# Contiguous x pieces, logit spectra stored by frequency and read back in whole rows, and three more weight tiles, in a Fourier layer with a soft mixture of experts

## The chip, the core and the metric

One core of a Trainium2 chip runs the program. The metric is the device time of one execution in microseconds, median of several runs. TensorE (PE in the profile; its weight loads are PEld), VectorE (DVE), ScalarE (ACT) and GpSimd (POOL) compute; SyncE (SP) issues nearly all DMAs, in program order, from one queue. Sixteen DMA engines move the data.

## What is computed

```python
X = np.fft.rfft(x, axis=1)                      # x: 8 batches, 2496 tokens, 256 channels
Yr = Xr @ w_r - Xi @ w_i + b_r
Yi = Xr @ w_i + Xi @ w_r + b_i
Y  = soft_threshold(Yr, 0.01) + 1j * soft_threshold(Yi, 0.01)
y  = np.fft.irfft(Y, n=2496, axis=1)            # all 19968 tokens from here on
logits = y @ phi                                # 32 slots: 8 experts, 4 slots each
d = softmax(logits, over tokens); slot_input = d.T @ y
slot_out[e] = relu(slot_input[e] @ w1[e]) @ w2[e]   # w1: 256x1024, w2: 1024x256 per expert
out = softmax(logits, over slots) @ slot_out
```

## The kernel before

The length 2496 is 39 times 64, and the transform is done in two factors. For each batch, `a_unit` (L322) loads x in pieces of a few columns on 120 partitions, splits each piece in a high and a low part (`xh` on ACT or DVE, `xl` on POOL) and multiplies by the 39-point matrix; the result goes through `ast` to a DRAM scratch `adr` and comes back turned round as `ap` (`load_ap`, L383). `f2` does the 64-point part, `lin_k` and `lin_y` the channel matrices, then the soft threshold gives `rt`. There are 40 such steps, five groups of four frequencies for each of eight batches, and TensorE is kept busy with step s while the other engines prepare step s+1. In time units of the program a step is 4, a batch 20, and `TB` = 166 is the start of the tail after the last step; every piece of work is a generator that yields its due time, and the program text of each engine is written in the order of those times (`heapq`, L750 to L759). So each engine works in a fixed order, and an instruction that waits holds back all that stands behind it on its engine.

The inverse transform of the output is never formed. Instead the logits are found in the frequency domain: `tp_p` (L484) multiplies the thresholded spectrum by `phi`, 32 values per frequency, and collects them in `p_sb`. `c_stages` (L604) then does, for each of batches 0 to 6:

1. `pg` = the inverse 64-point matrix `sinv` times `p_sb`, copied by ACT to `g_sb`: 128 partitions by 20 frequencies by 32 slots.
2. one DMA writes `g_sb` to a DRAM scratch `gd`, laid out as 64 tokens by 40 (real or imaginary part and frequency) by 32 (L618 and L619).
3. four DMAs read `gd` as `gp`, 120 partitions (three groups of tokens, times 40) by 22 by 32: two of 40x22 pieces, one of 40x20 and one of 40x2 pieces, every piece being 32 numbers or 128 bytes (L622 to L633). The third group has 20 tokens of its own, and its last two columns repeat its first two.
4. `halves` (L578) splits `gp` in two halves: `chpL` on ACT, `clpL` on DVE, and then three products by the 39-point matrix `m2` on TensorE give `pL`, which ACT copies to `L`, the logits by token. In batch 6 and in the last batch there is no split, and TensorE reads `gp` itself.
5. from `L`: the running maximum (`mx`, `pm`, `pb`), the exponentials `ee`, the way back to the frequencies (`pe`, `ea`, DMA to `ed`, two DMAs back as `eb`, `pd`, `dd`), and the weighted sum `pr` over the spectra `T`, which gives the slot inputs.

`last_chain` (L924) is the same for batch 7, without TensorE work to hide it: `g_sb` is written in three pieces of 12, 4 and 4 frequencies as they come (L927 to L936). Then the slot inputs go through the experts (`hps`, `po`; weights `w`), and 78 blocks of output are made (`pq`, `ost`).

The weights of the experts are 32 tiles of 512 KB, loaded by `load_w` (L843) in the order of the table `wl` in `PLAN` (L143): each entry is a due time relative to `TB` and a letter for the pool that the tile takes: `r` and `a` reuse tiles of the loads, `t` is a tile of the tail pool `tw` (10 tiles, `NTA` from `"nw"`, L148), `x` and `T` are pairs of half tiles that reuse working tiles, `h` are tiles of the pool `hl`.

All DMAs named here are issued by SP, and SP waits in line: `gp` is not issued before `gd` has landed, and what stands behind `gp` (the next `xr` and `adr`) not before `gp` is issued.

Of the kernel before, what the change touches and what calls it, by code (L numbers as in the profile page):

```python
# [11 lines left out]
F32 = mybir.dt.float32  # L12
# [18 lines left out]
GP = 2  # L31
# [18 lines left out]
def _constants():  # L50
    n1 = np.arange(N1)
    k1 = np.arange(K1)
    a39 = 2 * np.pi * (np.outer(n1, k1) % N1) / N1
    c39, s39 = np.cos(a39), np.sin(a39)
    s39[:, 0] = 0.0
    a64 = 2 * np.pi * (np.outer(np.arange(N2), np.arange(N2)) % N2) / N2
    q = np.outer(np.arange(N2), np.arange(N2)) % N2
    c64, s64 = np.cos(a64), np.sin(a64)
    c64[(q == 16) | (q == 48)] = 0.0
    s64[(q == 0) | (q == 32)] = 0.0  # L60

# [26 lines left out]
    smov = smov.reshape(128, K1 + 1, 64)
    smov = np.concatenate([smov[:, : KG + 1], smov[:, :1], smov[:, KG + 1 :]], axis=1).reshape(128, -1)
    sinv = suni[np.arange(128).reshape(2, N2).T.reshape(-1)].T  # L90
    sgn = np.ones((2, N2, K1))
    sgn[1] = sig.T
    sgn = sgn.reshape(128, K1)
    dsc = sgn * wk[None, :]

    ident = np.eye(128)
    dmask = np.tile(np.eye(32), (4, 4))
    f1a = f1.reshape(P1, R, 2, NGRP, KG).transpose(0, 3, 2, 4, 1).reshape(P1, Q1)
    f1 = f1.reshape(P1, R, 2 * K1).transpose(0, 2, 1).reshape(P1, Q1)
# [12 lines left out]
    return {k: np.ascontiguousarray(v.astype(np.float32)) for k, v in out.items()}
# [27 lines left out]
    "to": 0.7,  # L140
    "ws": [-29, -28.9, -28.8, 2],
    "late": {'6': {'cms': [19.75, 19.71, 860.75, 862, 864, 865], 'pd': [20.36, 20.37], 'pr': [31.55, 31.6, 31.65, 31.7, 31.75], 'pL': [5.4, 5.8], 'pm': 6.875, 'pb': 7.325, 'pe': [8.75, 9.75], 'pg': [0.875, 1.275], 'fr': {'sinv': 0, 'm2': 0, 'f1': 0, 'suni': 0}}, '5': {'pg': [1.1, 1.8], 'pL': [4.95, 5.75], 'pm': 6.8, 'pb': 7.15, 'pe': [9.2, 9.9], 'pd': [13.8, 14.8], 'pr': [15.0, 17.25, 19.5, 21.75, 24.0]}, '4': {'pr': [18.4, 20.49, 24.49, 28.49, 32.49]}},
    "T_": {'wl': [[-45, 'r'], [-44, 'r'], [-43, 'r'], [-31.0, 't'], [-30.7, 't'], [-29.4, 't'], [-27.6, 't'], [-27.8, 't'], [-11, 'a'], [-10.3, 'a'], [-9.6, 'a'], [-7.5, 'x'], [-6.4, 'x'], [1.11, 'x'], [1.07, 'h'], [1.08, 'h'], [1.09, 'h'], [1.1, 'h'], [1.11, 'h'], [13.55, 'h'], [13.1, 'h'], [13.6, 'h'], [13.6, 'h'], [13.61, 't'], [13.61, 't'], [13.61, 't'], [13.61, 't'], [13.61, 't'], [13.7, 'T'], [13.7, 'T'], [13.7, 'T'], [13.7, 'T']], 'cl': 16, 'cp': 46.5, 'ct': 46.6, 'du': [[-4.5, 0], [-2.4, 0], [1.2, 0]], 'd1': [5, 2, 4, 0, 0, 0], 'cm': [19.9, 19.91, 19.92, 25, 25.1, 25.2], 'cm7': [18, 20, 22, 23, 25, 27], 'ye': 0.2, 'te': [[5.6, 0.2], [5.5, 0.4]], 'pg': [-7, -3.25, -0.35], 'yt': 0.5, 'wr': -30.6, 'tp': [0, 0.9, 1.05, 0.5], 'tt': [[-0.4, 0.5, 0.6, 0.7, 0.8], [12, 12.1, 12.2, 12.3, 12.4]], 'z': 13.55, 'th': [0.1, 0.12], 'tl': [0.2, 0.25]},  # L143
    "f1": [1.5, 2.15],
    "kw": [[-40, 9]],
    "ap1": 1.85,
    "f0": 0.2,
    "nw": [3, 10, 9],  # L148
    "te": 'A',
    "tp": [0.5, 1.0, 1.9, 1.8],  # L150
    "tt": [2, 2.5],
# [29 lines left out]
def fourier_soft_moe_kernel(ctx: ExitStack, tc: tile.TileContext, t: dict, out: bass.AP):  # L181
    nc = tc.nc
# [3 lines left out]
    dr = ctx.enter_context(tc.tile_pool(name="dr", bufs=2, space=bass.MemoryType.DRAM))  # L186
# [46 lines left out]
    def sp(**kw):  # L233
        tc.keep_in_program_order(nc.sync.dma_start(**kw))  # L234
# [13 lines left out]
    def split(dst_h, dst_l, src, eh, el):  # L248
        copy(eh, dst_h, src)
        el.tensor_tensor(out=dst_l, in0=src, in1=dst_h.bitcast(F32), op=ALU.subtract)  # L250

    def load_x(i):
        if i >= len(xorder) or xorder[i] in xrs:
            return
        b, g = xorder[i]
        ng = min(xc, G - g)
        xr = wtile([PX, xc, D], F32, "xr", f"xr{b}_{g}")
        sp(out=xr[:, :ng, :], in_=x[b, :, g : g + ng, :])
        xrs[(b, g)] = xr

    def load(name, shape, pool=cons, eng=None):
# [316 lines left out]
    def halves(n, t0, times, out, const, fr, src, evac):  # L578
# [13 lines left out]
        for h in range(2):  # L592
# [8 lines left out]
            yield t0 + times[h] + 0.25  # L601
            evac(h, out[1](ps))

    def c_stages(b):  # L604
        ct_ = "ps"
        K_ = dict(PLAN, **PLAN["late"].get(str(b), {}))
# [8 lines left out]
            lambda h, ps: A.copy(out=g_sb[:, h * 10 : h * 10 + 10, :].rearrange("p k s -> p (k s)"), in_=ps),  # L615
        )
        yield t0 + K_["pg"][1] + 0.35
        gd = dr.tile([N2, 2 * K1, S], F32, tag="gd", name=f"gd{b}")  # L618
        sp(out=gd.rearrange("n (c k) s -> (n c) k s", c=2), in_=g_sb)  # L619
        yield t0 + K_["pg"][1] + 0.9  # L620
        gp = wtile([Q1, G, S], F32, "gp", f"gp{b}")
        for r in range(R):  # L622
            ge = 22 if r < 2 else 20
            p0 = r * 2 * K1
            sp(
                out=gp[p0 : p0 + 2 * K1, :ge, :],
                in_=gd[22 * r : 22 * r + ge].rearrange("g k s -> k g s"),
            )
            if ge < G:
                sp(  # L630
                    out=gp[p0 : p0 + 2 * K1, ge:, :],
                    in_=gd[22 * r : 22 * r + G - ge].rearrange("g k s -> k g s"),
                )  # L633
# [290 lines left out]
    def last_chain():  # L924
        b = B - 1
        for (k0, k1), tk in zip(((0, 12), (12, 16), (16, 20)), T_["pg"]):
            ks = slice(k0, k1)  # L927
            n = (k1 - k0) * S
            yield TB + tk
            if k0 == 0:  # L930
                g_sb = wtile([128, K1, S], F32, "g7", f"g_sb{b}")
                gd = dr.tile([N2, 2 * K1, S], F32, tag="gd", name=f"gd{b}")
            ps = psum("pf", f"pg{b}_{k0}")
            mm(out=ps[:, :n], lhsT=sinv, rhs=psb[b][:, ks, :], start=True, stop=True)
            A.copy(out=g_sb[:, ks, :].rearrange("p k s -> p (k s)"), in_=ps[:, :n])
# [3 lines left out]
        for r in range(R):
            ge = 22 if r < 2 else 20  # L940
            p0 = r * 2 * K1
            sp(
                out=gp[p0 : p0 + 2 * K1, :ge, :],
                in_=gd[22 * r : 22 * r + ge].rearrange("g k s -> k g s"),
            )
            if ge < G:
                sp(
                    out=gp[p0 : p0 + 2 * K1, ge:, :],
                    in_=gd[22 * r : 22 * r + G - ge].rearrange("g k s -> k g s"),
                )  # L950
# [310 lines left out]
```

## Time and profile before

| | |
|---|---|
| median of 3 runs | 580.69 us (577.52 to 581.72) |
| the profiled execution | 575.19 us |
| its span, first to last instruction | 573.4 us |
| busy: PE, DVE, ACT, POOL | 528.8, 419.3, 298.6, 281.0 us |
| mean granted TensorE clock | 0.971 |
| DMA | 118.55 MB, 207 GB/s over the span |

The profile's page shows the span in forty slices of 14.3 us. The stretch table gives, for a window, each engine's busy time, the DMA engines' mean busy share and the rate. The timeline lists instructions by start, with a bracket that tells how long the engine was idle before and what ended that. The chain of waits follows the work that ended last back to its start. DMA issues stand in the timeline as SPq with the time that SP took to issue them; when one has landed is seen from the instruction that waited for it.

### The profile page before, as it was taken

What the parts mean: (1) busy time and instruction counts of PE and PEld (TensorE: products, weight loads), DVE (VectorE), ACT (ScalarE), POOL (GpSimd) and SP (SyncE); (2) the same over time, 40 slices, a digit from 0 to 9 for tenths busy, and PEclk for the clock granted to TensorE, in tenths of its full rate; (3) what the DMA queues carried; (4) which work ended last, traced back from release to release, by engine and by line L of the source; (5) the groups of instructions that cost most, each with busy time, mean ns of one, the idle gap of its engine ahead of it and who ended that gap; (6) DMA issues with size and microseconds to landing.
All of it is one profiled execution on the core that took longest, in us unless ns stands there. A gap on an engine that the chain in (4) does not pass through costs nothing.

```text
span 573.4 us, 11788 instructions
## 1 busy us (share of the span) xinstructions
PE 528.8 (92%) x4358; PEld 447.4 (78%) x4358; DVE 419.3 (73%) x837; ACT 298.6 (52%) x650; POOL 281.0 (49%) x258
## 2 busy tenths in 40 slices
PE   8668999999999999999999999998899989799894
PEld 4357999989898879889988888897687767367673
DVE  0254988789979897989689977986776764247783
ACT  4334555667566656665665656553333333037662
POOL 0035778667676666658655865773445412000100
PEclk9887999999999999999999999998989999999897
DMA  8779878667776858775787577866624489969898
GB/s 241 235 259 241 198 162 175 156 171 178 205 176 178 173 154 204 170 180 156 177 196 187 151 179 185 238 184 193 164 80 102 121 199 298 369 218 363 330 374 352
DMA packets 92884, 118.55 MB, mean 207 GB/s; under 512 B 46802, under 2 KB 68624, under 8 KB 92828
## 3 DMA queue, kind: packets, MB, share of 16 engines
q1 hardware_dynamic: 92572, 116.73, 73.0%
q10 hardware_dynamic: 256, 1.08, 0.5%
q8 instruction: 34, 0.56, 0.4%
q14 instruction: 22, 0.18, 0.1%
HBM read 68.42 MB, written 49.38 MB: 205 GB/s over the span
## 4 chain that ended last, share of the span: by engine, by line
PE 65%; DMA 14%; DVE 12%; ACT 3%; issue 2%; SPq 2%; POOL 0%; ACTq 0%; DVEq 0%; POOLq 0%
PE py L240 15%; PE px L240 10%; PE pq L240 8%; PE pk L240 7%; PE pa L240 7%; PE pt L530 4%; DMA gp<-gd 3%; DMA gd<-g_sb 3%; PE pr L240 3%; DMA ap<-adr 2%; SPq L234 2%; PE pc L1065 2%; DMA eb<-ed 2%; DMA xr<-in_x 2%; DVE mx L177 1%
## 5 line engine op out<-in xcount | busy, mean ns | idle before, releaser
L177 POOL TENSOR_TENSOR rt<-ut,rt 128x512 f32<-128x512 f32 x79 | 111.7, 1414 | 26.5 <-DVE rt L177 22.0
L177 POOL TENSOR_TENSOR xsl<-xsm,xsh 128x256 fp32r<-128x256 f32 x77 | 59.4, 772 | 107.3 <-DVE xsh L177 72.5
L177 POOL TENSOR_TENSOR xl<-xr,xh 117x512 fp32r<-117x512 f32 x73 | 98.4, 1349 | 21.8 <-ACT xh L177 13.8
L240 PE MATMUL px<-smov,ap 128*128 128x128 f32 x640 | 86.8, 280 | 5.7 <-DMA ap<-adr 3.9
L240 PEld LDWEIGHTS px<-smov,ap 128*128 128x128 f32 x640 | 81.5, 195 | 11.6 <-issue 4.7
L177 ACT COPY ast<-pa 120x512 f32<-120x512 f32 x86 | 50.6, 588 | 69.7 <-PE pa L240 68.1
L177 ACT CAST xth<-px 128x512 fp32r<-128x512 f32 x80 | 46.9, 586 | 74.0 <-PE py L240 38.2
L177 DVE SCALAR_TENSOR_TENSOR ut<-py,pk,k 128x256 f32<-128x256 f32 x160 | 69.5, 475 | 16.7 <-PE py L240 12.4
L177 DVE TENSOR_TENSOR xtl<-px,xth 128x512 fp32r<-128x512 f32 x80 | 54.6, 683 | 24.7 <-ACT xsm L177 22.6
L240 PE MATMUL py<-xth,nwsh 128*128 128x256 f32 x160 | 54.0, 337 | 0.0
L177 DVE TENSOR_SCALAR rt<-ut 128x512 f32<-128x512 f32 x69 | 53.3, 772 | 0.5
L240 PE MATMUL pk<-xsh,w_rh 128*128 128x256 f32 x160 | 49.3, 308 | 2.0 <-DVE xsh L177 2.0
L530 PE MATMUL pt<-pk,rt 128*128 128x128 f32 x320 | 45.9, 273 | 0.9 <-DVE dd L177 0.6
L177 ACT COPY T<-pt 128x512 f32<-128x512 f32 x70 | 42.0, 599 | 9.0 <-PE pt L530 7.0
L240 PE MATMUL pk<-xsl,w_rh 128*128 128x256 f32 x160 | 46.2, 289 | 0.0
L240 PE MATMUL pk<-xsh,w_rl 128*128 128x256 f32 x160 | 46.1, 288 | 0.0
L240 PE MATMUL py<-xtl,wdh 128*128 128x256 f32 x160 | 45.3, 283 | 0.0
L240 PE MATMUL py<-xth,wdl 128*128 128x256 f32 x160 | 45.2, 283 | 0.0
L240 PE MATMUL py<-xth,nwsl 128*128 128x256 f32 x160 | 45.2, 283 | 0.0
L240 PE MATMUL py<-xth,wdh 128*128 128x256 f32 x160 | 45.2, 282 | 0.0
L240 PE MATMUL py<-xtl,nwsh 128*128 128x256 f32 x160 | 45.1, 282 | 0.0
L240 PE MATMUL pq<-rhs,ct 128*128 128x512 f32 x156 | 43.1, 416 | 0.3 <-DVE ost L177 0.3
(186 smaller groups left out, 1245.8 us busy)
## 6 DMA issues: line engine op xcount, KB each, us to landing
ap<-adr SPq DMA_DIRECT2D x76, 256.0 KB
out<-ost SPq DMA_DIRECT2D x37, 512.0 KB
xr<-in_x SPq DMA_DIRECT2D x35, 480.0 KB
adr<-ast SPq DMA_DIRECT2D x20, 720.0 KB
w<-in_moe_w SPq DMA_DIRECT2D x25, 512.0 KB
adr<-ast SPq DMA_DIRECT2D x8, 480.0 KB
w<-in_moe_w SPq DMA_DIRECT2D x14, 256.0 KB
x<-in_x SPq DMA_DIRECT2D x11, 240.0 KB
```

What stands on the lines that cost most here:

```text
L177: return lambda *a, **k: self.tc.keep_in_program_order(f(*a, **k))
L234: tc.keep_in_program_order(nc.sync.dma_start(**kw))
L240: tc.keep_in_program_order(nc.tensor.matmul(**kw))
L530: tc.keep_in_program_order(nc.tensor.transpose(out=out, in_=in_, identity=identity))
L1065: nc.tensor.transpose(out=pc[:, i * P1 : (i + 1) * P1], in_=chls[b][x][:, 2 * (r + i) : 2 * (r + i) + 2].rearrange("p g h s -> p (g h s)") ...
```

## The change

Three things are changed together.

**x in DRAM.** Before, x lay as 120 rows of 22 columns by 256 for each batch, so that a piece of 4 columns is 120 rows of 4 KB, 22 KB apart. Now each piece lies by itself, without gaps; the DMAs have the same rows and the same bytes.

**gd and gp.** `gd` now is laid out part, frequency, token, slot. Two DMAs write it, one for each part, in pieces of 128 bytes (64 partitions by 20 pieces); in the last batch that is six DMAs for three. A row of `gd` (one part and frequency, 64 tokens) is contiguous, so `gp` is read in two DMAs of whole rows: one for the first two groups of tokens (2 by 40 rows of 704 numbers, into 80 partitions) and one for the third group (40 rows of 640 numbers). The third group stands first in `gp` (`m2` and `sinv` are permuted to fit), and its two repeated columns are copied on chip by ACT (`gp_wrap`), due 0.91 units before the logits' products, and 0.1 units before them in the last batch.

**Weights.** The pool `tw` has 13 tiles for 10; the SBUF comes from a smaller descriptor scratch. Three `t` loads are added at -24, -22 and -20; the two `x` loads at -7.5 and -6.4 are gone, three `x` loads stand at 1.12, 1.13 and 13.55, and some `h`, `t` and `T` loads behind them change places.

```diff
-    m2 = m2.reshape(Q1, P1)
+    m2 = m2[[2, 0, 1]].reshape(Q1, P1)
...
-    "nw": [3, 10, 9],
+    "nw": [3, 13, 9],
...
+    def x_piece(b, g, n):
+        return x[b, g * PX * D : (g + n) * PX * D].rearrange("(p g d) -> p g d", p=PX, d=D)
...
-        sp(out=xr[:, :ng, :], in_=x[b, :, g : g + ng, :])
+        sp(out=xr[:, :ng, :], in_=x_piece(b, g, ng))
...
+    def gd_write(gd, g_sb, k0, k1):
+        for c in range(2):
+            sp(out=gd[c, k0:k1].rearrange("k n s -> n k s"), in_=g_sb[c * N2 : c * N2 + N2, k0:k1, :])
+
+    def gp_read(gp, gd):
+        rows = gd.rearrange("c k n s -> (c k) (n s)")
+        q = 2 * K1
+        sp(
+            out=gp[q:].rearrange("p g s -> p (g s)"),
+            in_=rows[:, : 2 * G * S].rearrange("q (r x) -> r q x", r=2),
+        )
+        sp(out=gp[:q, : G - 2, :].rearrange("p g s -> p (g s)"), in_=rows[:, 2 * G * S :])
+
+    def gp_wrap(gp):
+        A.copy(out=gp[: 2 * K1, G - 2 :, :], in_=gp[: 2 * K1, :2, :])
...
-        gd = dr.tile([N2, 2 * K1, S], F32, tag="gd", name=f"gd{b}")
-        sp(out=gd.rearrange("n (c k) s -> (n c) k s", c=2), in_=g_sb)
+        gd = dr.tile([2, K1, N2, S], F32, tag="gd", name=f"gd{b}")
+        gd_write(gd, g_sb, 0, K1)
         yield t0 + K_["pg"][1] + 0.9
         gp = wtile([Q1, G, S], F32, "gp", f"gp{b}")
-        for r in range(R):
...
+        gp_read(gp, gd)
         L = wtile([P1, G, S], F32, "L", f"L{b}")
+        yield t0 + K_["pL"][0] - PLAN["cl"][0] - 0.01
+        gp_wrap(gp)
...
-            sp(out=gd.rearrange("n (c k) s -> (n c) k s", c=2)[:, ks, :], in_=g_sb[:, ks, :])
+            gd_write(gd, g_sb, k0, k1)
...
+        yield TB + 6.9
+        gp_wrap(gp)
         yield TB + 7
```

SP around the round trip of batch 0, before and with the change (`ap_4` is a load of the running step, `xr_4` a piece of x, `adr_601` a write of the first factor):

```order
L234 DMA gd_1290<-g_sb_1178 128x640
L234 DMA ap_4_1315<-adr_182 64x4x256 x2
L234 DMA gp_1326<-gd_1290 40x22x32 x2
L234 DMA gp_1326<-gd_1290 40x20x32
L234 DMA gp_1326<-gd_1290 40x2x32
L234 DMA xr_4_1332<-in_x 120x1024
L234 DMA adr_601<-ast_18_1295 120x1024
```

```order
L234 DMA gd_1290<-g_sb_1178 64x20x32 x2
L234 DMA ap_4_1316<-adr_182 64x4x256 x2
L234 DMA gp_1327<-gd_1290 80x1x704
L234 DMA gp_1327<-gd_1290 40x640
L234 DMA xr_4_1331<-in_x 120x1024
L234 DMA adr_601<-ast_18_1296 120x1024
```

One write became two, four reads became two, and the order around them is the same. Batches 1 to 6 differ in the same way.

SP in the last batch, before and with the change, from the read of batch 6's `eb` to that of batch 7's `gp` (`w` are weight tiles):

```order
L234 DMA eb_6370<-ed_6353 64x20x32 x2
L234 DMA w_0_6425<-in_moe_w 128x512
L234 DMA w_1_6426<-in_moe_w 128x512
L234 DMA gd_6432<-g_sb_6431 128x384
L234 DMA w_0_6439<-in_moe_w 128x512
L234 DMA w_1_6440<-in_moe_w 128x512
L234 DMA gd_6432<-g_sb_6431 128x128 x2
L234 DMA gp_6540<-gd_6432 40x22x32 x2
```

```order
L234 DMA eb_6376<-ed_6359 64x20x32 x2
L234 DMA gd_6434<-g_sb_6433 64x12x32 x2
L234 DMA gd_6434<-g_sb_6433 64x4x32 x4
L234 DMA gp_6541<-gd_6434 80x1x704
L234 DMA gp_6541<-gd_6434 40x640
```

The two weight tiles between the writes are gone from here, and three writes became six. A third weight load, which stood between the `ed` write and the `eb` read of the last batch, now stands behind that read.

ACT in batch 6, before and with the change, around the new copy (`lg_1` and `L` feed TensorE's next products and the logits):

```order
L177 COPY xsm_3_1_6188<-px_3_1_6169 128x256 [waits Pool_49]
L177 COPY lg_1_6209<-pq_1_6193 128x128 [waits PE_49]
L177 COPY L_6120<-pL_0_6220 117x352 [waits PE_49]
L177 COPY L_6120<-pL_1_6223 117x352 [waits PE_49]
L177 CAST xth_4_0_6249<-px_4_0_6227 128x512 [waits PE_49,Activation_49]
```

```order
L177 COPY xsm_3_1_6193<-px_3_1_6174 128x256 [waits Pool_49]
L177 COPY gp_6122<-gp_6122 40x64 [waits DMAHW4_49]
L177 COPY lg_1_6215<-pq_1_6199 128x128 [waits PE_49]
L177 COPY L_6125<-pL_0_6226 117x352 [waits PE_49]
L177 COPY L_6125<-pL_1_6229 117x352 [waits PE_49]
L177 CAST xth_4_0_6255<-px_4_0_6233 128x512 [waits PE_49,Activation_49]
```

The copy waits for a DMA and stands ahead of `lg_1`. In batches 0 to 5 it stands straight ahead of the casts `chpL`. Nothing else moves on ACT, and nothing on DVE, POOL and TensorE but which weight tile has two halves.

More of the change, by code (lines that the diff above doesn't have):

```diff
@@ L89, in _constants @@
     smov = np.concatenate([smov[:, : KG + 1], smov[:, :1], smov[:, KG + 1 :]], axis=1).reshape(128, -1)
-    sinv = suni[np.arange(128).reshape(2, N2).T.reshape(-1)].T
+    sinv = suni.T
     sgn = np.ones((2, N2, K1))
@@ L142 @@
     "late": {'6': {'cms': [19.75, 19.71, 860.75, 862, 864, 865], 'pd': [20.36, 20.37], 'pr': [31.55, 31.6, 31.65, 31.7, 31.75], 'pL': [5.4, 5.8], 'pm': 6.875, 'pb': 7.325, 'pe': [8.75, 9.75], 'pg': [0.875, 1.275], 'fr': {'sinv': 0, 'm2': 0, 'f1': 0, 'suni': 0}}, '5': {'pg': [1.1, 1.8], 'pL': [4.95, 5.75], 'pm': 6.8, 'pb': 7.15, 'pe': [9.2, 9.9], 'pd': [13.8, 14.8], 'pr': [15.0, 17.25, 19.5, 21.75, 24.0]}, '4': {'pr': [18.4, 20.49, 24.49, 28.49, 32.49]}},
-    "T_": {'wl': [[-45, 'r'], [-44, 'r'], [-43, 'r'], [-31.0, 't'], [-30.7, 't'], [-29.4, 't'], [-27.6, 't'], [-27.8, 't'], [-11, 'a'], [-10.3, 'a'], [-9.6, 'a'], [-7.5, 'x'], [-6.4, 'x'], [1.11, 'x'], [1.07, 'h'], [1.08, 'h'], [1.09, 'h'], [1.1, 'h'], [1.11, 'h'], [13.55, 'h'], [13.1, 'h'], [13.6, 'h'], [13.6, 'h'], [13.61, 't'], [13.61, 't'], [13.61, 't'], [13.61, 't'], [13.61, 't'], [13.7, 'T'], [13.7, 'T'], [13.7, 'T'], [13.7, 'T']], 'cl': 16, 'cp': 46.5, 'ct': 46.6, 'du': [[-4.5, 0], [-2.4, 0], [1.2, 0]], 'd1': [5, 2, 4, 0, 0, 0], 'cm': [19.9, 19.91, 19.92, 25, 25.1, 25.2], 'cm7': [18, 20, 22, 23, 25, 27], 'ye': 0.2, 'te': [[5.6, 0.2], [5.5, 0.4]], 'pg': [-7, -3.25, -0.35], 'yt': 0.5, 'wr': -30.6, 'tp': [0, 0.9, 1.05, 0.5], 'tt': [[-0.4, 0.5, 0.6, 0.7, 0.8], [12, 12.1, 12.2, 12.3, 12.4]], 'z': 13.55, 'th': [0.1, 0.12], 'tl': [0.2, 0.25]},
+    "T_": {'wl': [[-45, 'r'], [-44, 'r'], [-43, 'r'], [-31.0, 't'], [-30.7, 't'], [-29.4, 't'], [-27.8, 't'], [-27.6, 't'], [-24, 't'], [-22, 't'], [-20, 't'], [-11, 'a'], [-10.3, 'a'], [-9.6, 'a'], [1.07, 'h'], [1.08, 'h'], [1.09, 'h'], [1.1, 'h'], [1.11, 'h'], [1.12, 'x'], [1.13, 'x'], [13.55, 'x'], [13.6, 'h'], [13.6, 'h'], [13.6, 'h'], [13.6, 'h'], [13.61, 't'], [13.61, 't'], [13.61, 't'], [13.61, 't'], [13.61, 't'], [13.7, 'T']], 'cl': 16, 'cp': 46.5, 'ct': 46.6, 'du': [[-4.5, 0], [-2.4, 0], [1.2, 0]], 'd1': [5, 2, 4, 0, 0, 0], 'cm': [19.9, 19.91, 19.92, 25, 25.1, 25.2], 'cm7': [18, 20, 22, 23, 25, 27], 'ye': 0.2, 'te': [[5.6, 0.2], [5.5, 0.4]], 'pg': [-7, -3.25, -0.35], 'yt': 0.5, 'wr': -30.6, 'tp': [0, 0.9, 1.05, 0.5], 'tt': [[-0.4, 0.5, 0.6, 0.7, 0.8], [12, 12.1, 12.2, 12.3, 12.4]], 'z': 13.55, 'th': [0.1, 0.12], 'tl': [0.2, 0.25]},
     "f1": [1.5, 2.15],
@@ L273, in load_x0 @@
         xr = wtile([PX, GP, D], F32, "T", f"x0_{g}")
-        sp(out=xr, in_=x[0, :, g : g + GP, :])
+        sp(out=xr, in_=x_piece(0, g, GP))
         x0.append(xr[:P1])
@@ L617, in c_stages @@
         yield t0 + K_["pg"][1] + 0.35
-        gd = dr.tile([N2, 2 * K1, S], F32, tag="gd", name=f"gd{b}")
-        sp(out=gd.rearrange("n (c k) s -> (n c) k s", c=2), in_=g_sb)
+        gd = dr.tile([2, K1, N2, S], F32, tag="gd", name=f"gd{b}")
+        gd_write(gd, g_sb, 0, K1)
         yield t0 + K_["pg"][1] + 0.9
         gp = wtile([Q1, G, S], F32, "gp", f"gp{b}")
-        for r in range(R):
[L623 to L633, printed above, removed]
+        gp_read(gp, gd)
         L = wtile([P1, G, S], F32, "L", f"L{b}")
+        yield t0 + K_["pL"][0] - PLAN["cl"][0] - 0.01
+        gp_wrap(gp)
         yield from halves(
@@ L931, in last_chain @@
                 g_sb = wtile([128, K1, S], F32, "g7", f"g_sb{b}")
-                gd = dr.tile([N2, 2 * K1, S], F32, tag="gd", name=f"gd{b}")
+                gd = dr.tile([2, K1, N2, S], F32, tag="gd", name=f"gd{b}")
             ps = psum("pf", f"pg{b}_{k0}")
@@ L935, in last_chain @@
             A.copy(out=g_sb[:, ks, :].rearrange("p k s -> p (k s)"), in_=ps[:, :n])
-            sp(out=gd.rearrange("n (c k) s -> (n c) k s", c=2)[:, ks, :], in_=g_sb[:, ks, :])
+            gd_write(gd, g_sb, k0, k1)
         yield TB + 1
         gp = wtile([Q1, G, S], F32, "gp", f"gp{b}")
[L939 to L950, printed above, removed]
+        gp_read(gp, gd)
         L = wtile([P1, G, S], F32, "L", f"L{b}")
         mx = wtile([P1, 4, S], F32, "mx", f"mx{b}")
+        yield TB + 6.9
+        gp_wrap(gp)
         yield TB + 7
@@ L1211, in _prep @@
     rows = np.arange(PX) % P1
-    arrays["x"] = np.asarray(inputs["x"])[:, _tokens()[rows]]
+    xt = np.asarray(inputs["x"])[:, _tokens()[rows]]
+    arrays["x"] = np.stack([
+        np.concatenate([xt[b, :, g : g + n].reshape(-1) for g in range(0, G, n)])
+        for b, n in enumerate([GP] + [2 * GP] * (B - 1))
+    ])
     for nm in ("moe_w1", "moe_w2"):
@@ L1250 @@
     )
-    nc = _bacc.Bacc("TRN2", target_bir_lowering=False, num_devices=1)
+    nc = _bacc.Bacc("TRN2", target_bir_lowering=False, num_devices=1, dynamic_dma_scratch_size=1024)
     t = {
```

## The prediction

> **What bounds the kernel now.** I read the page first, then the stretch table, then the timelines of the two round trips that the change rewrites, and last the chain of waits for the head.
>
> ```profile
> span 573.4 us, 11788 instructions
> PE 528.8 (92%) x4358; PEld 447.4 (78%) x4358; DVE 419.3 (73%) x837; ACT 298.6 (52%) x650; POOL 281.0 (49%) x258
> ```
>
> TensorE is busy for 92%. Where TensorE has no gaps, a transfer matters only through what makes TensorE wait, so the stages have to be told apart.
>
> ```profile
> 0.00:60.00 60.00, 47.66 (x227) 34.28 (x228) 21.56 (x46) 24.93 (x47) 16.63 (x21) 0.89 0.86 244
> 60.00:107.00 47.00, 47.00 (x420) 43.39 (x419) 39.86 (x79) 27.06 (x60) 35.77 (x32) 1.00 0.71 164
> 107.00:127.00 20.00, 19.19 (x166) 17.27 (x165) 15.71 (x33) 11.91 (x26) 11.74 (x12) 1.00 0.74 184
> 380.00:405.00 25.00, 22.16 (x189) 19.79 (x189) 17.72 (x39) 11.14 (x26) 11.63 (x13) 0.93 0.59 161
> 405.00:436.00 31.00, 28.45 (x247) 24.17 (x249) 23.22 (x49) 9.57 (x24) 15.00 (x16) 0.89 0.51 135
> 462.00:513.00 51.00, 43.54 (x440) 28.28 (x439) 21.89 (x51) 13.71 (x34) 3.65 (x9) 1.00 0.90 286
> ```
>
> Each row gives the window, its length, the busy time of PE, PEld, DVE, ACT and POOL, the granted clock, the DMA share and GB/s. TensorE idles 12.3 us in the first 60, 0.8 around batch 0's round trip (107 to 127), 2.8 around batch 5's (380 to 405) and 7.5 in the tail (462 to 513); between these it has nothing to give back. So a later `gp` in batches 0 to 4 costs TensorE what goes beyond its slack there, and a faster `gp` gains nothing.
>
> **The round trip in batch 0.** SP's timeline, then the part of the full timeline that `gp` releases:
>
> ```profile
> 107.23 0.35 SPq L234 DMA_DIRECT2D gd<-g_sb  x1
> 111.23 3.32 SPq L234 DMA_DIRECT2D gp<-gd  x4
> 115.03 0.41 SPq L234 DMA_DIRECT2D adr<-ast  x1
> 120.98 1.24 SPq L234 DMA_DIRECT2D ap<-adr  x2
> 135.25 0.32 SPq L234 DMA_DIRECT2D ed<-ea  x1
> 138.09 1.38 SPq L234 DMA_DIRECT2D eb<-ed  x2
> ```
>
> ```profile
> 116.31 0.88 ACT L177 CAST chpL<-gp 120x352 fp32r<-120x352 f32 x2 [0.82 <-DMA gp<-gd]
> 117.09 0.58 ACT L177 CAST xth<-px 128x512 fp32r<-128x512 f32 x1
> 117.93 0.41 PE L240 MATMUL pL<-chpL,m2h 120*117 120x352 f32 x1
> 118.50 0.29 PE L240 MATMUL py<-xth,nwsh 128*128 128x256 f32 x1
> ```
>
> The write takes 4.0 us until SP may issue the reads, the reads 5.1 until ACT starts. ACT already waits 0.8 for them, TensorE does not: it needs `chpL` at 117.93, and a cast takes half of 0.88, so the slack is 1.6 less 0.5, or 1.1 us. Behind the cast on ACT stand `xth`, `xsm` and `T`; TensorE needs `xth` soon after `pL`, so they have about the same slack.
>
> **The price of the new transfers.** The rates come from stretches in which one kind of transfer is alone:
>
> ```profile
> 441.50:442.50 1.00, 1.00 (x13) 0.61 (x6) 0.46 (x2) 0.00 (x0) 0.61 (x1) 1.00 0.86 135
> 475.00:480.00 5.00, 4.38 (x28) 3.19 (x26) 2.49 (x9) 2.07 (x6) 0.00 (x0) 1.00 1.02 389
> 4.00:8.00 4.00, 4.00 (x12) 2.24 (x12) 0.00 (x0) 1.17 (x2) 0.00 (x0) 1.00 0.94 288
> 35.50:37.00 1.50, 1.50 (x15) 1.50 (x14) 0.88 (x2) 0.12 (x1) 0.89 (x1) 1.00 0.74 280
> ```
>
> In the first, `gp`'s 128-byte pieces move: 135 / (0.86 x 16) = 9.8 GB/s for a busy engine. In the second, whole 4 KB rows of weights: 389 / (1.02 x 16) = 23.8.
>
> *Write.* 327,680 bytes in 128-byte pieces over 16 engines take 327.7 / (16 x 9.8) = 2.1 us, against 0.86 in today's rows of 2,560 bytes: +1.2. The second issue hides behind the data. This takes the price of a 128-byte read for a write, which no row here shows; below, today's 0.86 (no loss), and above, twice the read's price, 4.2.
>
> *Read.* A `gp` DMA has a fixed part: `ed<-ea` lands 2.84 after its issue, with 337,920 bytes on at most 15 engines (120 rows), 0.95 us; that leaves 1.9. An issue with three dimensions, as `ap`'s, takes 0.6 for 0.3. What decides is over how many engines the first read's 225,280 bytes go. No view shows a DMA's engines one by one; the bounds are 16 engines, 0.6 us, and one, 9.5. The nearest row is the last one above: there `adr` is written in DMAs of 72 rows, more are queued, and the engines are busy to 0.74 only, which is twelve of sixteen, the largest number up to 16 that divides 72; weights, with 128 rows, reach 1.02. The count of the outermost dimension thus sets the number of engines. The new read's source has 2 outermost (2 by 40 rows) and its destination 80; a share has to be whole on both sides, so I take two engines: 225.3 / (2 x 23.8) = 4.7 us. The second read (40 rows, so ten engines) includes these two, behind the first: 10.2 KB each, 0.4. Together 1.9 + 0.3 + 4.7 + 0.4 = 7.3 against 5.1: +2.2.
>
> On this the Trainium skill has a rule, in "DMA: Bandwidth & Descriptors", section "Why a DMA increments its semaphore by 16 and not by 1": the number of engines is the largest up to 16 that divides the slowest dimension, other than one, of both access patterns. The 0.74 agrees for 72 rows; that both sides count, and that 2 against 80 gives two, no row of this run shows. By the rule the read's data takes the 4.7 us, and with all engines it would take 0.6.
>
> *Copy.* ACT copies 40x64 once both reads are there:
>
> ```profile
> L177 ACT COPY zrow<-dd 1x128 f32<-1x128 f32 x8 | 2.4, 294 | 4.3 <-DVE dd L177 4.3
> ```
>
> +0.3. So `chpL` starts 1.2 + 2.2 + 0.3 = 3.7 us later. Less the slack of 1.1, TensorE waits 2.6 at `pL`; I give back 0.5, since VectorE and ACT catch up meanwhile and later waits shrink. 2.1 for each of batches 0 to 4: **+10.5**. On the two engines that read, the following `adr` is held up too, and `ap` behind it (120.98), by up to 2 us; the wait at `pL` covers that, and without this cover it would be paid. SP itself waits 1.2 longer for the write, but issues two reads in 1.0 us for four in 3.3, so that `xr` and `adr` leave it earlier than now.
>
> **Batches 5 to 7.** From SP's and TensorE's timelines:
>
> ```profile
> 380.90 0.35 SPq L234 DMA_DIRECT2D gd<-g_sb  x1
> 381.31 0.42 SPq L234 DMA_DIRECT2D adr<-ast  x1
> 383.15 4.83 SPq L234 DMA_DIRECT2D gp<-gd  x4
> 439.78 2.67 SPq L234 DMA_DIRECT2D gp<-gd  x4
> 464.87 0.99 SPq L234 DMA_DIRECT2D gd<-g_sb  x2
> 468.41 2.85 SPq L234 DMA_DIRECT2D gp<-gd  x4
> 484.00 1.39 SPq L234 DMA_DIRECT2D eb<-ed  x2
> ```
>
> ```profile
> 390.63 0.64 PE L240 MATMUL pL<-chpL,m2h 120*117 120x352 f32 x1 [2.38 <-ACT chpL L177]
> 444.43 0.82 PE L240 MATMUL pL<-gp,pk 120*117 120x352 f32 x2
> 447.33 0.91 PE L240 MATMUL px<-smov,ap 128*128 128x128 f32 x6 [0.58 <-DMA ap<-adr]
> 473.38 1.41 PE L240 MATMUL pL<-gp,pk 120*117 120x352 f32 x4 [2.37 <-DMA gp<-gd]
> 490.37 1.31 PE L240 MATMUL pd<-eb,pk 128*128 128x320 f32 x4 [3.08 <-DMA eb<-ed]
> ```
>
> Batch 5 has no slack: TensorE waits 2.4 already, since the reads stand behind an `adr` write. Read data today is 337.9 / (10 x 9.8) = 3.4 behind it, then 5.1: +1.7, with write and copy **+3.2**. Batch 6: read 4.65 today, 7.3 then, +2.65, write +1.2, copy +0.3; the 0.58 at `px` is swallowed: **+3.6**. The copy also holds `lg_1` on ACT, but its product stands behind `pL` on TensorE. Batch 7: the last piece is ready at about 465.5, but six issues of 0.6 have to leave SP, so the last write lands 0.7 later; read 4.97 to 7.3, copy 0.3: **+3.3**.
>
> **Weights.** The earlier loads go into the stretch from 405 to 436, where the DMA engines are busy to 0.51, at no cost; their products are not waited for now. A 512 KB load before `eb` in batch 7 is gone, 524 / 381 = 1.4 us of every engine; `eb` needs 5.7 from its second issue to `pd`, and I take **-0.5** (0 to -1.4). The two tiles gone before `gd` leave the writes issue-bound.
>
> **Head.** The chain of waits:
>
> ```profile
> 4.79 7.01 DMA x<-in_x
> 11.82 9.63 DMA xr<-in_x
> 21.59 3.61 PE pa L240 x4
> 39.45 4.11 DMA ap<-adr
> 43.70 2.04 PE px L240 x8
> ```
>
> The head is a queue of transfers up to 43.70. x alone moves at 288 GB/s with share 0.94 (4 to 8): 19.1 for a busy engine, against 23.8 for the gapless weights. The rows are alike, so the 22 KB between them is what differs. Ahead of `ap` at 39.45 stand 11 pieces of 240 KB and three of 480 KB, 4.18 MB: 14.5 us at 288, 11.7 at 23.8 x 15 = 357: **-2.8** (0, if the gap is not the cause, to -4.5, if what follows on SP moves up too). Later x pieces are hidden by TensorE.
>
> **Sum.** 10.5 + 3.2 + 3.6 + 3.3 - 0.5 - 2.8 = +17.3 on the span of 573.4 and the execution of 575.2. That one lies 5.5 below the median of the runs, 580.69; I add the sum to the median: **598.0 us**.
>
> **Rivals.** *The first read goes wide.* If ten or more engines share it, the round trip takes 1.9 + 0.3 + 0.6 to 0.9 and the second issue, about 3.5 for 5.1; that pays for the write and the copy, TensorE's slack takes the rest, and the head and `eb` are left: -3.3, about 577, a little faster. It decides as soon as the read lands before about 3.7 us. For it: 80 partitions on the destination's side. Against it: the outer 2.
>
> *Half is hidden.* Two engines, but TensorE's slack in batches 0 to 4 reaches to the next need of `L` and `xth`, and only 1 us is paid in each, 2 in batches 5 to 7: 5 + 6 - 3.3 = +7.7, 588. For it: ACT is 52% busy. Against it: the engines' orders are fixed, and `pL` has to run.
>
> *The small writes cost double.* 4.2 us of data instead of 2.1, with nothing left of slack, in eight batches: +17 more, 615 at most; half of that, 606, is the likelier. The Trainium skill speaks for it on the same page, section "Specifications": 512 bytes are the least for line rate, and below that the engine reads, changes and writes. By that rule the write would be the 4.2; no run here shows such a write yet.
>
> *No gain in the head* would add 2.8 to any of these.
>
> **Chances.** Two engines with the wait paid 0.60; wide read 0.18; half hidden 0.14; double write 0.08. The first lies in 591 to 604 by itself. The range goes from 576, where most of the wide read's case is in, to 607, with half of the double write's. A measurement here tells about 1%, 5.8 us, from no change. Faster by more than that, below 574.9, is a part of the wide read's case only, with some luck in the head: 0.12. Within 1%: the rest of that case and the lower part of the half-hidden one, 0.18. Slower: 0.70.
>
> **What would show it.** `gp<-gd` x2 for x4 on SP, with ACT's new copy waiting until about 7 us after the first of them, in every batch; `pL` with 2 to 3 us of TensorE idle ahead of it in batches 0 to 4; the DMA share falling to a few tenths while the first read runs alone in the tail; 4:8 with well over 288 GB/s, and `px` of 43.70 some 3 us earlier. It is wrong if the copy waits less than 4 us after the read's issue, or if TensorE has no gap at `pL`.

## The result, and the profile after

The change made the kernel slower: 624.19 us (median of 4 runs, 621.5 to 627.74) against 579.28 for the kernel before on the same chip (also of 4), a ratio of 1.082 (95% interval 1.077 to 1.087). Forecast were 598.0, and a range that ended at 607. The direction was right, and so was the transfer that I blamed; the size was not: the sum said +17.3, and the span grew by 622.9 - 573.4 = 49.5.

The head of the profile's page, then the row of spans and clocks:

```profile
span 622.9 us, 11776 instructions
PE 544.2 (87%) x4358; PEld 457.0 (73%) x4358; DVE 414.1 (66%) x837; ACT 298.9 (48%) x658; POOL 279.5 (45%) x258
```

```profile
core 0: 622.9 us, clock 0.943
```

TensorE has the same 4358 matmuls, but it is busy 15.4 us longer (528.8 before): the same products run slower. Its idle time grew by 34.1 (78.7 for 44.6); the two make the 49.5. The longer busy time goes with the clock. It was 0.971 of 573.4, so 16.6 us of clock were withheld; now it is 0.057 x 622.9 = 35.5.

The round trip of batch 0, in the timeline of SP and then in that of all engines:

```profile
111.41 1.80 SPq L234 DMA_DIRECT2D gd<-g_sb  x2
...
116.29 1.19 SPq L234 DMA_DIRECT2D gp<-gd  x2
```

```profile
124.81 0.24 ACT L177 COPY gp<-gp 40x64 f32<-40x64 f32 x1 [5.14 <-DMA gp<-gd]
124.96 0.87 ACT L177 CAST chpL<-gp 120x352 fp32r<-120x352 f32 x2
...
125.49 0.64 PE L240 MATMUL pL<-chpL,m2h 120*117 120x352 f32 x1 [3.14 <-ACT chpL L177]
```

The write takes 4.9 us until the reads go out (4.0 before), the reads 8.5 until the copy starts (5.1 before), and TensorE, which had 1.1 us to spare here, idles 3.14. The product itself is slower too, 0.64 us for 0.41. TensorE's waits over the span, as total, number and longest:

```profile
PE pL L240 <- ACT chpL L177: 24.6, 6, 6.6
PE pL L240 <- DMA gp<-gd: 13.8, 2, 7.4
```

That is 38.4 us ahead of `pL` in the eight batches (by batch 3.1, 2.6, 3.1, 4.8, 4.4, 6.6, 6.5, 7.4), against 2.38 and 2.37 in batches 5 and 7 before: 33.6 us more. 49.5 less 33.6 leaves 16 us. They stand behind the waits, in the stretch table (the third column from the right is the granted clock):

```profile
125.00:129.00 4.00, 3.51 (x16) 3.42 (x17) 3.12 (x7) 3.36 (x9) 1.85 (x2) 0.57 0.10 30
303.00:309.50 6.50, 4.49 (x19) 4.41 (x20) 3.34 (x8) 4.08 (x10) 2.84 (x3) 0.50 0.22 68
422.00:430.00 8.00, 4.29 (x22) 4.12 (x23) 3.82 (x9) 2.83 (x8) 1.74 (x2) 0.57 0.33 96
480.00:490.00 10.00, 4.87 (x14) 3.22 (x15) 1.53 (x2) 1.31 (x4) 0.94 (x1) 0.51 0.53 136
517.50:525.00 7.50, 4.80 (x16) 3.58 (x16) 1.51 (x5) 1.15 (x3) 0.00 (x0) 0.54 1.03 364
```

Each wait is followed by a stretch at about half clock in which TensorE does have work. The stretches of 107 to 127 and 462 to 513 in the table of before had 1.00. The head gained nothing, the `px` of 43.70 comes at 46.14:

```profile
4.00:8.00 4.00, 4.00 (x11) 2.31 (x10) 0.00 (x0) 0.85 (x2) 0.00 (x0) 1.00 0.97 268
```

x moves at 268 GB/s for 288. One sign that I had named did not show either: from 513 to 519, while the first read of the last batch runs, the DMA share is 0.82 and not a few tenths, for SP issues eight weight tiles right behind the reads.

So there were two theories to test: **A**, the first read runs on two engines because its source has 2 outermost, and the rest is the clock that its waits bring down; **B**, the small writes, one large DMA as such, or SP's queue make the loss. The terms for x and for the weights could each be run alone.

### The profile page after: what moved, and what is told of

The parts are those of the page before. It is cut to its first block, busy times and chain, and to the rows that moved or that the text cites. A ratio compares the mean times of both kernels' runs of the same rounds, so it can differ in the third digit from the quotient of the medians.

```text
span 622.9 us, 11776 instructions
## 1 busy us (share of the span) xinstructions
PE 544.2 (87%) x4358; PEld 457.0 (73%) x4358; DVE 414.1 (66%) x837; ACT 298.9 (48%) x658; POOL 279.5 (45%) x258
## 4 chain that ended last, share of the span: by engine, by line
PE 57%; DMA 24%; DVE 8%; ACT 4%; issue 3%; SPq 2%; POOL 1%; ACTq 0%; POOLq 0%
PE py L240 14%; DMA gp<-gd 10%; PE px L240 8%; PE pq L240 7%; DMA gd<-g_sb 6%; PE pa L240 6%; PE pk L240 5%; PE pt L533 3%; DMA xr<-in_x 3%; PE pL L240 3%; PE pr L240 2%; SPq L234 2%; DMA adr<-ast 2%; PE pc L1066 2%; PE pe L240 1%
## 5 line engine op out<-in xcount | busy, mean ns | idle before, releaser
L177 DVE TENSOR_SCALAR rt<-ut 128x512 f32<-128x512 f32 x69 | 52.0, 754 | 0.5
L240 PE MATMUL py<-xth,nwsl 128*128 128x256 f32 x160 | 46.5, 291 | 0.0
L240 PE MATMUL py<-xth,wdh 128*128 128x256 f32 x160 | 46.5, 291 | 0.0
L240 PE MATMUL py<-xtl,nwsh 128*128 128x256 f32 x160 | 46.5, 290 | 0.0
```

What stands on the lines that cost most here:

```text
L177: return lambda *a, **k: self.tc.keep_in_program_order(f(*a, **k))
L240: tc.keep_in_program_order(nc.tensor.matmul(**kw))
```

## The experiments

### x alone, and the weights alone

The kernel before with only `x_piece` and its host layout:

```diff
-        sp(out=xr[:, :ng, :], in_=x[b, :, g : g + ng, :])
+        sp(out=xr[:, :ng, :], in_=x_piece(b, g, ng))
...
```

> The kernel before with the contiguous x pieces alone; gd, gp and the weights as before. My forecast's term: the 22 KB between the rows of x costs DMA time, so the head is 2.8 us shorter, about -0.5% of 579, and 4:8 moves more than 288 GB/s. Rival, from the changed kernel's trace, where x's eleventh piece landed at 14.82 us for 13.86 and TensorE reached the px of 43.70 only at 46.14: the rows of 4 KB cost the same wherever they lie, and the head is 0 to 3.7 us longer, 0 to +0.6%. A time at or above that of the kernel before, with 4:8 at 288 GB/s or less, takes the term away.

576.78 us, ratio 0.9993 (0.9961 to 1.0024): nothing. The stretch table of this kernel:

```profile
4.00:8.00 4.00, 4.00 (x10) 2.34 (x10) 0.00 (x0) 0.59 (x1) 0.00 (x0) 1.00 0.97 266
```

The rows are no faster for lying together. The term of -2.8 is gone, and the longer head in the changed kernel's trace is not x's doing either: in a later run with the same x (the exchanged loops, below) 4:8 moved 283 GB/s, and the `px` of 43.70 came at 43.38.

The kernel before with only the new table and its 13 tiles:

```diff
-    "nw": [3, 10, 9],
+    "nw": [3, 13, 9],
...
```

> The kernel before with the three further weight tiles and the new table alone; x, gd and gp as before. My forecast's term: -0.5 us (0 to -1.4), since the 512 KB load ahead of eb in batch 7 is gone and the earlier loads lie where the DMA engines are busy to 0.51: 577 to 580, not to be told from no change. Rival: the three loads at -24 to -20 collide with the round trips of batches 5 and 6 (the wait at pL of batch 5 is 2.38 us now) and cost 2 to 5 us.

575.03 us, ratio 0.9966 (0.9937 to 0.9995): a small gain, about 2 us. In its trace the last batch's reads go out 4.6 us after the first write for 5.5, and TensorE waits 0.80 at `pL` there for 2.37.

### The outermost dimension of the first read

Three reads of 40 rows for the two, in the changed kernel:

```diff
-            in_=rows[:, : 2 * G * S].rearrange("q (r x) -> r q x", r=2),
+        for r in range(2):
...
+                in_=rows[:, r * G * S : r * G * S + G * S],
...
```

> The changed kernel with its first read of 80 rows as two DMAs of 40 rows, so that no access pattern has an outer 2; same bytes, same rows, one DMA more. Theory A, the outer 2 puts two thirds of gp on two engines: by the estimate of 1.0 for the issues, 1.9 fixed and 338 KB over ten engines at 23.8 GB/s, 1.4, the trip from the first issue to pL is about 4.3 us for 8.2; the idle of TensorE ahead of pL (3.1, 2.6, 3.1, 4.8, 4.4, 6.6, 6.5 and 7.4 us in batches 0 to 7) falls by 3.9 in each or to 0, and with it the half clock behind it: 624 - 30 to 40 = 584 to 594. Rival B, the loss comes from the writes in 128-byte pieces and the longer queue on SP, and the number of engines matters little: no more than 8 us come back, 616 or more.

586.58 us, ratio 1.0171 (1.0129 to 1.0212): 38 us are back. But this also made two DMAs of one. The next kernel keeps the changed kernel's two DMAs, with their bytes and rows, and only exchanges the source's outer loops (the rows of `m2` are put in the new order, here and with 4 outermost):

```diff
...
-            in_=rows[:, : 2 * G * S].rearrange("q (r x) -> r q x", r=2),
+            in_=rows[:, : 2 * G * S].rearrange("q (r x) -> q r x", r=2),
```

> The changed kernel with the two outer loops of the first read's source exchanged (40 rows outermost, then 2 groups, instead of 2 and then 40) and the rows of m2 permuted to fit. The number of DMAs, their bytes and the length of their rows are those of the changed kernel. Theory A, the outermost count of 2 sets two engines: with 40 outside the trip from the first issue to pL falls as it did with three reads, from 8.5 to 9.6 us to 4.7 to 6.5, and less by the one issue that is saved, 0.4: 583 to 588, at or a little under the 586.58 of three reads. Rival B, one large DMA is slow as such (what helped there was a third DMA): the time stays at 615 or more, and the copy waits 8 us after the issue.

585.48 us, ratio 1.0126 (1.0081 to 1.0172). Its timelines of SP and of ACT in batch 0:

```profile
111.44 1.40 SPq L234 DMA_DIRECT2D gp<-gd  x2
```

```profile
116.29 0.24 ACT L177 COPY gp<-gp 40x64 f32<-40x64 f32 x1 [1.46 <-DMA gp<-gd]
```

The copy starts 4.85 us after the issue for 8.52. The two letters exchanged in one pattern are worth 1.0818 - 1.0126 = 6.9%, or 38.7 us between the medians. Between the two, three reads with 4 outermost:

```diff
-                in_=rows[:, r * G * S : r * G * S + G * S],
+                in_=rows[:, r * G * S : r * G * S + G * S].rearrange("(q a) x -> a q x", a=4),
```

> As the run with three reads, but each of the two reads of the first groups goes through its 40 rows as 4 by 10 (outermost 4), with the rows of m2 permuted to fit; third read as before. Between two and ten engines. Theory A, the outermost count is the number of engines and the data time goes by rows per engine: with two engines the read landed 8.1 us after its issue in batch 0 (40 rows of 2,816 bytes for each engine at 112 ns, 4.5, beside a fixed 3.6), with ten 4.15 (8 rows, 0.9, beside 3.25). With four, 20 rows, 2.2: the second read lands about 5.5 to 5.8 after the first issue and the wrap copy starts at 5.8 to 6.3, some 0.8 to 1.2 later than with ten; TensorE's slack in batches 0 to 4 is used up, and 5 to 7 pay: 590 to 596. Rival B, only an outermost count of 2 is special, by a different path for it: 584 to 588 as with three reads.

598.67 us (median of three runs, 590.69 to 599.25), ratio 1.0332 (1.0268 to 1.0396). SP and ACT, batch 0:

```profile
115.52 1.91 SPq L234 DMA_DIRECT2D gp<-gd  x3
```

```profile
121.05 0.25 ACT L177 COPY gp<-gp 40x64 f32<-40x64 f32 x1 [2.17 <-DMA gp<-gd]
```

Over the eight batches the copy starts 5.4 to 7.3 us after the issue (mean 6.1), with three reads of ten 4.3 to 5.8 (5.1), in the changed kernel 8.4 to 9.5 (8.6). So 2 is no special path; the trip gets shorter as the count goes up, and B fails as the main cause (the small write is priced next). The time is 3 us above the 590 to 596 that I expected, with one of the three runs at its lower end; the head of the profiled run was longer as well (TensorE waited 6.5 us for `ap`, 4.2 with three reads).

The trace also keeps a list of the DMA packets, with the start, duration and size of each. It bears the count out: while the first read moves, its rows of 2,816 bytes are most often in flight two at a time in the changed kernel (66 to 89% of that stretch in the eight batches), four at a time with 4 outermost (in seven of the eight), and about ten at the height with the loops exchanged and with three reads. The Trainium skill has the rule in "DMA: Bandwidth & Descriptors", section "Why a DMA increments its semaphore by 16 and not by 1": the largest number up to 16 that divides the slowest dimension of both sides. These three counts, against the same 40 or 80 rows on the other side, agree with it.

### The small write alone

The kernel before, with `gd`'s rows 160 bytes apart, so that its one write goes in pieces of 128 bytes:

```diff
-        gd = dr.tile([N2, 2 * K1, S], F32, tag="gd", name=f"gd{b}")
+        gd = dr.tile([N2, 2 * K1, S + 8], F32, tag="gd", name=f"gd{b}")
...
```

> The kernel before, with the rows of gd padded from 128 to 160 bytes: the one write (128 partitions, all engines) goes in pieces of 128 bytes instead of 2,560; four reads in pieces of 128 bytes as before. It prices the small write by itself. My term: the write lands 1.2 us later; hidden in batches 0 to 4, 1.2 in each of 5 to 7: +3 to +4, 580 to 581 for 577, ratio 1.005 to 1.007. Rival, small writes cost double or more: 3.3 or more later, beyond the 1.1 to 1.5 us of slack in batches 0 to 4 as well: +15 or more, 592. Second rival, nothing: under +1. The time from gd's issue to gp's (4.0 us in batches 0 to 4, 2.25 in batch 5, 2.5 to 3.3 in batch 6) shows it directly.

590.86 us, ratio 1.0228 (1.0185 to 1.0271), +13. SP in batch 0 and in batch 5:

```profile
107.13 0.56 SPq L234 DMA_DIRECT2D gd<-g_sb  x1
...
112.31 3.62 SPq L234 DMA_DIRECT2D gp<-gd  x4
```

```profile
384.40 0.55 SPq L234 DMA_DIRECT2D gd<-g_sb  x1
...
388.89 4.08 SPq L234 DMA_DIRECT2D gp<-gd  x4
```

In batch 0 the reads go out 5.18 us after the write for 4.00: the +1.2 of my term, and batches 1, 2 and 4 are alike (+1.0 to +1.2). In batch 5 it is 4.49 for 2.25, in batch 6 5.72 for 3.33, in batch 3 6.51 for 4.06: +2.2 to +2.4. The packet list shows what differs. In batch 5 little else moves, and the 2,560 pieces take 2.35 us from the first to the last, where the wide rows took 0.97. In batch 0 the wide rows took 2.6 already, among rows of `adr`, and the pieces 2.9. In both some 0.9 comes on top, 0.4 before the first piece and 0.5 behind the last. In the mean of a batch a piece took 12.7 to 15.0 ns to write, and 13.0 to 14.2 to read in the kernel before: the small write costs what the small read does, as the sum assumed.

TensorE waits 5.1 us more at `pL` in this run (mostly in batches 5 to 7, with up to 0.36 in 0 to 4), and it is busy 535.3 us for 528.8 with the same products, at a clock of 0.965 for 0.971: together 11.6 of the 12.3 us by which the span is longer. The doubled data of the rival would have been 3.3 us more in every batch. The Trainium skill, on the same page, section "Specifications", has 512 bytes as the least for line rate; these runs show a price below it, but not the 4.2 us of that rival.

### The clock

Products of the identity ahead of the first `pL`, in the changed kernel, into the same tile of PSUM (the memory that TensorE writes to), where `pL` then overwrites them:

```diff
+            if n == "m2" and h == 0:
+                for _ in range(WARM[int(out[0][2:])]):
+                    mm(out=ps[:, :128], lhsT=ident, rhs=ident, start=True, stop=True)
...
```

> The changed kernel with products of the identity by itself (18, 18, 18, 32, 32, 48, 48 and 56 in batches 0 to 7; 0.12 us each by pt's rows, so 2.2 to 6.7 us) ahead of the first product of pL, in the time in which TensorE waits there; their results are overwritten. pL comes no earlier. Theory A: each of these waits is followed by 3.4 to 10.2 us of granted clock 0.5, and that costs TensorE some 1.3 us more in each of batches 0 to 7 beside the idle time, which is part of why my sum is too small: with the products the clock stays at 1.00 there, and 8 to 12 us come back, 612 to 616. Rival B: the half clock falls on work that waits for other engines anyway, and what I under-sized is the wait itself: 0 to 2 us come back, or some are lost where the products overrun the wait, 622 to 628.

627.15 us, ratio 1.087 (1.0827 to 1.0913). By the numbers that looks like rival B, but the test was spoilt: a product took 0.23 us and not 0.12, so they outlasted the waits: `pL` came 9.84 us after the reads' issue in batch 0 for 9.20, and 14.2 for 8.5 in batch 7, 23 us in all. That this cost only 3 us spoke for A. With about half as many:

> As the run before with products of the identity ahead of pL, but 10, 9, 10, 17, 16, 24, 24 and 28 of them in batches 0 to 7. In that run one product took 0.23 us (36 matmul instructions for 18 products in 4.18 us), not the 0.12 that I had reckoned with, so they overran each wait by 0.9 (batch 0) to some 5.5 us (batch 7), 20 to 25 us in all, at granted clock 1.00 in the waits, and the time was yet only 3 us above that of the changed kernel. Theory A, the half clock after the waits costs the rest of that, more than 8 us: with products that end inside the wait (2.1 to 6.4 us) the time falls from 624 to 604 to 614. Rival B, the clock does not matter: 622 to 626, as the wait itself stays.

608.03 us, ratio 1.0525 (1.0481 to 1.0569): 16 us less than the change, with the same reads. TensorE in batch 0, then the stretch table, the row of clocks, and TensorE's busy time with the share of the added products in it:

```profile
118.99 2.40 PE L241 MATMUL pL<-pk 128*128 128x128 f32 x20
122.66 0.42 PE L241 MATMUL pL<-chpL,m2h 120*117 120x352 f32 x1 [1.27 <-ACT chpL L178]
```

```profile
122.00:126.00 4.00, 3.34 (x21) 2.97 (x22) 3.33 (x8) 3.94 (x10) 1.69 (x2) 1.00 0.06 24
```

```profile
core 0: 604.4 us, clock 0.981
```

```profile
PE 560.8 (93%) x4634; PEld 475.8 (79%) x4634; DVE 414.2 (69%) x837; ACT 298.7 (49%) x658; POOL 280.0 (46%) x258
L241 PE MATMUL pL<-pk 128*128 128x128 f32 x276 | 32.2, 275 | 0.0
```

`pL` comes 8.8 to 10.5 us after the reads' issue, in the changed kernel 8.5 to 9.6; nothing was fetched sooner. Only the clock stayed up, and `pL` takes 0.42 us again for 0.64. Without the added products TensorE is busy 560.8 - 32.2 = 528.6 us, as in the kernel before (528.8) and 15.6 less than in the changed one. These are the 16 us that the waits did not explain. Does it hold for the kernel before, which had such waits too? There, products in four waits:

```diff
+BUSY = {'px0_2_0': 12, 'pL5': 9, 'pd5': 7, 'pc4_0': 7}
...
+    def busy(key, ps):
+        for _ in range(BUSY.get(key, 0)):
+            mm(out=ps[:, :128], lhsT=ident, rhs=ident, start=True, stop=True)
...
```

> The kernel before with nothing changed but the products of the identity in four waits (12 ahead of the px of 43.7 us, 9 ahead of pL and 7 ahead of pd in batch 5, 7 ahead of the fifth group of pc). With the weights as well it was 0.9882 of the kernel before, the weights alone 0.9966. If the two add up, 0.9916, about -4.9 us: the half clock by itself. If the weights were what made the difference, 0.998 or more.

572.27 us, ratio 0.9914 (0.9884 to 0.9944), clock 0.983: work that computes nothing makes the kernel 5 us faster.

### Versions

The kernel before with the weights and the four waits:

> The kernel before with the weight tiles of the change (which alone gave 575.03, ratio 0.9966) and with products of the identity in four waits of TensorE that a half clock follows there: 12 ahead of the px of 44.18 us (a wait of 3.07, then 6.8 us at 0.5), 9 ahead of pL in batch 5 (2.38; 3.4), 7 ahead of pd in batch 5 (1.77; 3.4) and 7 ahead of the fifth group of output transposes pc (1.90; 3.4), each 0.23 us, so 2.8, 2.1, 1.6 and 1.6 us. x, gd and gp as before. Theory A, the half clock costs time of its own: the 31.3 us at half clock fall by up to 17, and 3 to 7 us come back: 568 to 572. Rival B, TensorE's work behind these waits is waited for by nobody, or other engines set the pace there: 574 to 576.

570.82 us, ratio 0.9882 (0.9847 to 0.9917): faster than both kernels, and the sum of its parts (-2.0 and -5.0). The same two windows, first of the kernel before, then of this one:

```profile
42.00:49.00 7.00, 5.30 (x22) 5.01 (x23) 0.14 (x1) 1.97 (x4) 2.73 (x3) 0.51 1.01 266
388.00:396.00 8.00, 5.62 (x44) 5.25 (x33) 4.99 (x10) 3.57 (x9) 2.49 (x3) 0.79 0.56 152
```

```profile
42.00:49.00 7.00, 5.40 (x39) 4.73 (x38) 0.00 (x0) 3.51 (x8) 1.32 (x2) 1.00 0.98 274
388.00:396.00 8.00, 6.92 (x54) 6.02 (x51) 5.15 (x11) 3.46 (x9) 2.26 (x3) 1.00 0.52 136
```

Two waits more were no gain:

> As the run with weights and products in four waits (570.82), with two waits more: 12 products of f1a ahead of the pa of 20.9 us (a wait of 3.19, then 3.4 us at half clock) and 10 of the identity ahead of pd in batch 7 (2.74; 3.4). If the half clock costs 0.34 us per us wherever it stands, 2.3 us more: 568 to 569. If those two stretches are set by DMAs and by VectorE, nothing: 570 to 572.

574.78 us, ratio 0.9942 (0.9918 to 0.9967), worse than without them, at the same clock of 0.989. In its trace the loss lies in the head (the `px` of 43.52 comes at 45.04) and in batch 5; whether the products ahead of `pa` did it or the head's spread from run to run is open. And the change itself, with its loops exchanged and six waits filled:

> The changed kernel with the two loops of the first read exchanged (585.48) and products of the identity in six of the waits of TensorE that are left there: 12 ahead of the px of 43.4 us, 10 ahead of pL in batch 5, 8 ahead of pd in batch 5, 6 ahead of pL in batch 6, 13 ahead of pL and 11 ahead of pd in batch 7. Half-clock time was 35.7 us there, of which some 20 stand behind these waits; at 16.2 us for 47.6 us less, as the run with products that end inside the wait showed, 20 us are worth 6 to 7: 577 to 580, about the time of the kernel before. Rival: what is left of the loss is the small write's wait itself, and the products bring under 3: 583 to 586.

577.83 us, ratio 1.0026 (1.0001 to 1.0051): the time of the kernel before. With the weights and filled waits in both (six here, four there) the route by whole rows is 1.0026 - 0.9882 = 1.4% behind the old one. The small write alone, with its waits left empty, cost 2.3%; that the faster reads give part of it back is likely, but no run shows it by itself.

## Why the prediction failed

*The read, two engines.* The step held: the count of 2 decides, and widening it to ten takes 3.7 us from the trip in batch 0. The sum's own rate gives the same: 4.7 and 0.4 on two engines, 1.4 for the 327.7 KB of both reads on ten. Its data term was too small. The copy started 8.4 to 9.5 us after the issue, where the sum had 7.3: in batch 0 +3.4 for +2.2. The packet list divides these 8.5 us: 1.5 until the first row moves, 6.2 for the 80 rows, 0.4 until the second read is through, 0.5 until the copy starts. So the fixed part, 2.0 for 2.2, was right, and the rows took 5.9 to 6.9 us in the eight batches for 4.7. Half of them took 113 ns or less in batch 0, which by itself would make 4.5 us for the 40 of each engine, but the mean was 145. Other transfers ran meanwhile (DMA share 0.62 in 118 to 120, 0.90 in 120 to 122); that they held up the two engines is likely, and not shown.

*The write, +1.2.* The number came in batches 0, 1, 2 and 4 of the small write alone, but in batch 0 by luck: the sum had 1.2 of data, and there the data took 0.3 more, start and landing 0.9. In batch 5 the data took 1.4 more, near the term, and the 0.9, which no term had, made 2.2. The step took one price for a write that shares the queues and for one that has them nearly to itself. In batches 3 and 4 of the change the reads went out 6.6 and 6.4 us after the first write, for 4.9 to 5.3 in 0 to 2. There the write's pieces took 4.0 us for 2.7 to 3.0, with some 300 rows of `ap` among them for 27 in batch 0. Why `ap` came between them is open; in the run with half as many products both batches took 4.9.

*"I give back 0.5, since VectorE and ACT catch up."* This step failed, and with it the sum: nothing is given back, each wait is charged a second time. The forecast waits at `pL`, with 2.1 us in batches 0 to 4 and 3.2, 3.6 and 3.3 behind, come to 20.6; measured were 33.6, above all by the read: 8.6 in the mean for 7.3, in each of eight batches. The 16 us that the half clock cost were in no term and in no rival, though the rows that I quoted for other columns showed a clock of 0.89 in 0:60, 0.93 in 380:405 and 0.89 in 405:436, each of them with waits of 1.8 us or more. 33.6 + 16 makes the 49.5.

*Half hidden, double write, wide read.* The first two fell: TensorE had a gap in every batch, and the write did not double. The wide read, at 577, did not come, since its condition was not met; but where the exchange met it the time was 585.5 and not 577, because the trip took 4.3 to 5.5 us for the 3.5 of that sum, and the write and the clock cost more than it allowed.

*Head, -2.8, and weights, -0.5.* x alone changed nothing; the lower rate of x in the first microseconds was read as a price of the 22 KB between rows, from one row that did not vary that distance. The weights gave 2.0 (0.3 to 3.6): in the trace 1.6 of it is the wait at `pL` of the last batch, so the loads ahead of `gd` mattered, for whose going I had counted no gain.

## What to carry to other kernels

Read the outermost count of both access patterns before counting bytes: 2 by 40 rows and 40 by 2 rows are the same data, and here they differed by 39 us. A wait of 1.5 us or more on TensorE is to be priced with the half clock that may follow it, and where it cannot be removed, products that nobody reads may pay for themselves as long as they end before the wait does. A stage with slack hides a longer transfer only up to the slack: 3.4 us more on the reads and 0.9 on the write brought 3.1 of wait in batch 0.

## What the runs showed of the hardware

The granted clock was halved in stretches of 3.4 us or multiples of that. A row's length times the clock withheld, doubled, gives the time at half clock: 4.00 x 0.43 x 2 = 3.4 in 125:129, 8.00 x 0.43 x 2 = 6.9 in 422:430. The length of a wait alone does not decide. In the kernel before, two waits of 2.4 us, 2.38 in batch 5 and 2.37 in batch 7, went differently: the first is in the row 388:396 above, with 0.79 (3.4 us at half), the second here:

```profile
470.00:476.00 6.00, 3.54 (x24) 2.71 (x23) 2.88 (x6) 2.01 (x5) 0.00 (x0) 1.00 0.91 235
```

In the kernel with exchanged loops a wait of 1.52 in batch 6 was followed by 3.4 us at half, and one of 3.38 in batch 7 by none:

```profile
448.00:456.00 8.00, 6.14 (x30) 5.08 (x31) 3.29 (x7) 2.55 (x7) 3.24 (x3) 0.79 0.60 178
478.00:486.00 8.00, 5.27 (x31) 4.15 (x32) 3.19 (x10) 2.07 (x5) 0.00 (x0) 1.00 0.92 345
```

The Trainium skill ("TensorE: Matmul & The Clock Gate", section "HAM oscillation — how this bites in real kernels") warns of gaps above some 3.4 us; here waits of 1.5 to 3.1 did it. Per microsecond of clock withheld the cost was about 0.7: 35.5 to 11.5 us (604.4 x 0.019) for 16 us in the changed kernel, 16.6 to 9.7 (569.6 x 0.017) for 5 in the kernel before.
